# Swapping the two operands of a long convolution inside a gated attention and state-space kernel

## The chip, the core and the metric

The kernel runs on one core of a Trainium2 chip. The metric is the device time of one execution in microseconds. Three executions of the kernel before gave 949.06, 960.0 and 962.29 us, so their median is 960.0 us. The profiled execution is a fourth one and took 953.17 us.

## The reference, cut to what matters

```python
def reference(x, wqkv, wo, A, B, C, log_dt, Dskip, gate_w):      # x: 2048 x 512
    g = sigmoid((x * gate_w).sum(-1))
    a = attention(x, wqkv, 32 heads of 16) @ wo                   # softmax over all 2048 keys
    K[d, l] = Re sum_n C[d,n] * exp(dt[d]*A[d,n]*l) * dt[d]*B[d,n]   # 512 channels, 128 states
    y[l, d] = sum_{m<=l} K[d, m] * x[l-m, d]                      # causal, 2048 taps a channel
    return g * a + (1 - g) * (y + x * Dskip)
```

The reference does the convolution with Fourier transforms. The kernel does it directly, with matmuls.

## The kernel before, in words

Two problems share the core. **Attention** makes 2048 tiles of scores (4 heads side by side, 128 keys by 512 queries). A step, g, takes two or three of them: TensorE (PE) writes the scores into one of two PSUM tiles `SC0`, `SC1` (`qk`), ScalarE (ACT) takes their exponentials (`ex`, line 899, tile `ET`), and PE multiplies these by the values (`pv`, bank `OA`). There are 683 steps. From step 262 on VectorE (DVE) takes part of the exponentials with integer arithmetic (tiles `DZ`, `DU`), and a step then has two tiles on ACT and one on DVE. The queries for the next 16 steps come through `Qm` loads.

**The convolution** has two stages. The K stage (`table`, `kstage`) makes the 2048 taps of 32 channels, a block, 16 blocks in all: the tap at l = T*a + t is a product of a power for a and a power for t, summed over the states, so one matmul with 32 columns of `At` as weights and 64 or 48 columns of `PT` as moving operand makes them. T is 64: a runs over 32 partitions, t over 64 columns. `base_a`, `base_b`, `roots` and `factors` make the power tables on DVE (names beginning in L are small powers, in M large ones). The taps go out to DRAM (`kpd`) in rows of 2048 behind 32 zeros.

The Y stage (`ystage`) convolves. J = 32: output position l is cut into l = 32c + r, r on 32 partitions, c on 64 columns. For each channel 16 matmuls accumulate into bank `MB`: before, the weights are a 128 x 32 Toeplitz piece of the taps (`Kop`, loaded by `kloads` with overlapping rows, 8 channels to a load, three buffers) and the moving operand is the input `X` (32 channels a load, laid out with channels innermost, so that consecutive columns of one channel lie 32 elements apart). Four channels run side by side in the four column groups of the array: 512 matmuls a block, in groups of four. The bank `MB` is shared (a lock) by projections, K stage, Y stage and output projection.

**The order of the work** is written by a list scheduler in Python (`Sched`) while the program is recorded. It keeps a clock for each engine and adds a cost for each piece: `KMM` for a group of four K matmuls, `YMM` for a group of four Y matmuls, in us. After each step `fill` puts the waiting pieces of the other threads into the gaps that by these costs PE, DVE and the SP queue have; left-over gaps get matmuls on zeros (`wm`) that keep PE active. What is left when the steps have run out follows behind them. At run time each engine goes through its list strictly in order, so a matmul that waits holds up the scores behind it. All loads of both stages, and the `Qm` loads, go through the one SP queue in its order.

Of the kernel before, what the change touches and what calls it, by code (L numbers as in the profile page):

```python
# [13 lines left out]
P = 128  # L14
# [15 lines left out]
YAT = 140  # L30
XB = 32
XW = NC * XB
ZCOL = .216 / 512
# [24 lines left out]
VG = 4 * VW + 16  # L58
KMM = .055
YMM = .055  # L60
YSEG = 2
# [357 lines left out]
def declare(nc, es):  # L419
# [56 lines left out]
    for h in range(2):  # L476
        for n in ("L2", "L4", "L8", "L16", "L32", "L48", "M1", "M2", "M4", "M8", "M16", "M24", "W1"):
            sb(f"{n}.{h}", D, FP32)
        for n in (16, 32, 48):
            sb(f"DL{n}.{h}", 8 * D // 2)  # L480
        for n in (8, 16, 24):
            sb(f"DM{n}.{h}", 4 * D // 2)

# [10 lines left out]
    sb("sE", 16 * 32)  # L494
    sb("Kst", 2 * 512)
    for k in range(NK):
        sb(f"Kop{k}", KG * 512)
    for k in range(2):
        sb(f"X{k}", XW)
    sb("Yst", 2 * 512)  # L500
# [3 lines left out]
    B["MB"] = Buf("MB", "ps", 512, FP32)  # L504
    for n, free in (("kpd", D * KR), ("xrd", S * D), ("ytd", D * S), ("ybd", D * 512), ("qd", D * S), ("od", D * S)):
        B[n] = Buf(n, "dr", free, BF16)
        B[n].t = nc.dram_tensor("gm_" + n, [free // P, P], BF16)
# [95 lines left out]
def record(nc, p, B, ins):  # L603
# [51 lines left out]
    for n, s in (("BreT", "bre"), ("BimT", "bim"), ("CreT", "cre"), ("CimT", "cim")):  # L655
        load_par(n, ins[s])
    dma("SP", lambda e: e.dma_start(B["gwT"](0, [[1, 4]]), dap(ins["gw"], 0, [[1, P], [P, 4]]), allow_slow_non_contiguous=True),
        [], [(B["gwT"], 0)], lat=4)
    for k in range(D // XB):
        dma("SP", lambda e, k=k: e.dma_start(B["xrd"].dram(k * XW, [[XB, NC], [S * D // J, J], [1, XB]]),  # L660
                                             dap(x_t, (J - 1) * D + XB * k, [[J * D, NC], [-D, J], [1, XB]])), [], [(B["xrd"], k)], c=.6, lat=12)
    dma("SP", lambda e: e.dma_start(B["od"].dram(1536 * D, [[1, 512 * D]]), dap(x_t, 1536 * D, [[1, 512 * D]])), [], [(B["od"], 3)], c=.6, lat=6)
# [396 lines left out]
    def roots(h):  # L1059
        for o, x in (("L2", "L1"), ("L4", "L2"), ("L8", "L4")):  # L1060
            yield from cmul(o, x, x, h)
        for o, x, y in (("L16", "L8", "L8"), ("L32", "L16", "L16"), ("L48", "L16", "L32")):
# [4 lines left out]
        for o, x, y in (("M8", "M4", "M4"), ("M16", "M8", "M8"), ("M24", "M8", "M16")):  # L1067
            yield from cmul(o, x, y, h)
            yield from factors(o, h)

    def factors(n, h):
        l, d, z = B[f"{n}.{h}"], B[f"D{n}.{h}"], n[0] == "L"
# [53 lines left out]
    def base_a(pb):  # L1126
        At, h, d0 = B[f"At{pb}"], pb // 4, NP * (pb % 4)
        yield from powers(pb, FP, ((0, "W0"), (1, "W1")), ((2, "M2", None), (4, "M4", None)), True)
        yield ("DVE", .65)
        op("DVE", lambda v: v.tensor_copy(At(0, [[NA, 2], [2 * NA, NP], [1, 8]]), FP(0, [[e8, 2], [8, NP], [1, 8]])),  # L1130
           [(FP, 0)], [(At, 0)], c=.65)
        for m in range(1, 4):
            C = B[f"DM{8 * m}.{h}"]
            for ti, yr in ((v1, 0), (v2, 1)):
# [27 lines left out]
    def table(blk):  # L1162
# [8 lines left out]
        for m in range(1, 4):  # L1171
            Dm = B[f"DL{16 * m}.{h}"]
            for k in range(2):
# [10 lines left out]
    def skip():  # L1184
# [9 lines left out]
        yield ("SP", .6)  # L1194
        dma("SP", lambda e: e.dma_start(kpd.dram(0, [[4 * KR, P], [KR, 4], [1, J]]), wm(0, [[J, 4], [1, J]])), [(wm, 0)], [(kpd, "z")], c=.6, lat=4)

    def kstage(blk):
# [8 lines left out]
        for i in range(8):  # L1206
            yield ("PE", 4 * KMM)
            for x in range(2):
                for k in range(2):
                    n = T - 16 * k  # L1210
                    for j in range(4):
                        mm(lambda i=i, j=j, n=n: MB(64 * i + T - n, [[1, n]], 32 * j, 32),
                           lambda i=i, j=j, x=x: At(NA * (2 * (a0 + 4 * i + j) + x), [[1, NA]]),
                           lambda i=i, j=j, x=x, k=k, n=n: PT(k * PA + n * (2 * (4 * i + j) + x), [[1, n]]),
                           R, ky, False, x == k == 1, pos=(0, 32 * j), c=KMM if j == 0 else 0, a=n // 4, cfg="C")
        yield ("DVE", .7, -1)
        op("DVE", lambda v: v.tensor_copy(Kst(512 * (blk % 2), [[1, 512]]), MB(0, [[1, 512]])), ky, [(Kst, blk % 2, blk)], c=.66)  # L1217
# [9 lines left out]
    def kloads():  # L1227
        for v in range(D // KG):
            K, blk = B[f"Kop{v % NK}"], v * KG // CB
            yield ("AFTER", f"g{YAT}")  # L1230
            yield ("AFTER", f"kd{blk}")
            if v >= NK:
                yield ("AFTER", f"yv{v - NK}")
            for a in range(4):
                yield ("SP", .6)
                dma("SP", lambda e, a=a, v=v, K=K: e.dma_start(K(0, [[512, KG], [1, 512]], 32 * a, 32),  # L1236
                                                               kpd.dram(v * KG * KR + 1 + 512 * a, [[1, 32], [KR, KG], [1, 512]])),
                    [(kpd, (blk, j)) for j in range(4)] + [(kpd, "z")], [(K, a, v)], c=.62, lat=3.0)
            sch.mark(f"kl{v}")

    def xloads():
        yield ("AFTER", f"g{YAT}")
        for k in range(2):
            X = B[f"X{k}"]
            yield ("POOL", .3)
            op("POOL", lambda g, X=X: g.memset(X(0, [[1, XW]]), 0.0), [], [(X, a) for a in range(4)], c=4)
        for k in range(D // XB):
            X = B[f"X{k % 2}"]
            if k >= 2:
                yield ("AFTER", f"yu{XB * (k - 1) // CB - 1}")  # L1250
            for a in range(4):
                yield ("SP", .6)
                dma("SP", lambda e, a=a, k=k, X=X: e.dma_start(X(16 * a * XB, [[1, (NC - 16 * a) * XB]], 32 * a, 32),
                                                               B["xrd"].dram(k * XW, [[S * D // J, J], [1, (NC - 16 * a) * XB]])),
                    [(B["xrd"], k)], [(X, a, k)], c=.62, lat=3.0)
            sch.mark(f"xl{k}")

    Yst, ytd, ybd, Yl, Yb = B["Yst"], B["ytd"], B["ybd"], B["Yl"], B["Yb"]

    def ystage():  # L1260
        for u in range(NBLK):
            k, r2 = CB * u // XB, u % 2
            X = B[f"X{k % 2}"]
            yield ("AFTER", "gt")
            yield ("AFTER", f"xl{k}")
            yield ("AFTER", f"kl{CB * u // KG}")
            yield ("LOCK", "MB")
# [5 lines left out]
            for i in range(8):  # L1273
                v = (CB * u + 4 * i) // KG
                K = B[f"Kop{v % NK}"]
                R = [(K, a, v) for a in range(4)] + [(X, a, k) for a in range(4)]
                yield ("AFTER", f"kl{v}")
# [224 lines left out]

    for th, pr in ((norms(), 0), (qms(), 0), (projs(), 1), (gate(), .8), (ystage(), 2), (kloads(), 3), (space(), 2), (vscaled(0), 2.2), (vscaled(1), 2.2), (skip(), 1.9),
                   (xloads(), 4), (early(), 1.5), (reload(), 5), (outs(), 6)):
# [123 lines left out]
```

## Time and profile before

| | |
|---|---|
| profiled execution, device time | 953.17 us |
| its span, first to last instruction | 951.4 us |
| granted TensorE clock, mean | 0.937 |
| busy share: PE, DVE, ACT | 85%, 76%, 84% |
| exponential steps on ACT: first begins, last ends | 12.97 us, 866.8 us |

The span has three parts for this change. Up to step 140 (213.8 us) the convolution only makes tables. From step 140 its operands are loaded, and Y matmuls run among the steps. After the last step the rest of the convolution and the closing work run with ACT idle. Busy shares are means over all of these; what a stage costs has to be read in that stage.

### The profile page before, as it was taken

Reading aid. Unit: us, or ns where it says so; the run is one execution under the profiler, and the core shown is the slowest. Engines: PE = TensorE matmul, PEld = TensorE weight load, DVE = VectorE, ACT = ScalarE, POOL = GpSimd, SP = SyncE. Lnnn points to the kernel's source line nnn. Section 1 sums busy time; section 2 is a strip of 40 time slices with the busy share of each in tenths; the row PEclk is TensorE's granted clock in tenths of the full one; section 3 lists DMA queues with packets and bytes.
Section 4 is the critical chain, followed back from the end, with each engine's and each line's share of the span. In section 5 each row is a group of like instructions: output and inputs, shape, how many; then the busy total and the mean of one; then the engine's idle time right before and its main releaser. Section 6 shows DMA issues by size and latency. Waiting matters only on the chain.

```text
span 951.4 us, 35452 instructions
## 1 busy us (share of the span) xinstructions
PE 809.7 (85%) x16143; PEld 379.6 (40%) x16170; DVE 727.3 (76%) x1316; ACT 797.9 (84%) x694; POOL 13.4 (1%) x13
## 2 busy tenths in 40 slices
PE   7887777777888988998989989998999999999253
PEld 3222233322354555644544334343442444446150
DVE  5877999997969453786977989987899999983004
ACT  6996999999979886897979999997998999994000
POOL 5000000000000000000000000000000000000000
PEclk7877999999999998999989999999999999999676
DMA  8761000028175897776756414569553645456923
GB/s 188 73 52 8 16 11 13 16 56 185 38 164 117 173 189 147 165 143 132 159 120 132 81 33 94 112 110 170 113 116 75 143 99 114 97 116 138 172 59 112
DMA packets 202870, 101.10 MB, mean 106 GB/s; under 512 B 121424, under 2 KB 201168, under 8 KB 202704
## 3 DMA queue, kind: packets, MB, share of 16 engines
q1 hardware_dynamic: 200720, 97.65, 51.5%
q8 instruction: 127, 2.08, 1.0%
q10 hardware_dynamic: 2000, 1.18, 0.5%
q14 instruction: 23, 0.19, 0.1%
HBM read 83.40 MB, written 13.03 MB: 101 GB/s over the span
## 4 chain that ended last, share of the span: by engine, by line
PE 56%; ACT 28%; DMA 5%; DVE 4%; issue 4%; SPq 2%; ACTq 0%; DVEq 0%
ACT ET L899 28%; PE MB L619 25%; PE SC L619 16%; PE OA L619 15%; DMA gm_qd<-Qs 2%; DMA X<-gm_xrd 1%; SPq L1236 1%; DVE DZ L935 1%; DMA Wq<-in_A_wqkv_dram 1%; DVE OnT L989 1%; DMA Wo<-in_A_wo_dram 1%; DMA Kop<-gm_kpd 1%; DVE ON L982 0%; DMA Yl<-gm_ytd 0%; DVE DU L946 0%
## 5 line engine op out<-in xcount | busy, mean ns | idle before, releaser
L899 ACT ACTIVATE ET<-SC 128x1024 bf16<-128x1024 f32 (+1 forms) x683 | 789.9, 1337 | 65.2 <-PE SC L619 59.1
L619 PE MATMUL SC<-Qm,KT 32*128 32x512 bf16 x2048 | 281.4, 397 | 57.6 <-ACT ET L899 46.8
L619 PE MATMUL MB<-X,Kop 128*32 128x49 bf16 (+15 forms) x8192 | 269.7, 281 | 35.1 <-DMA X<-gm_xrd 17.3
L935 DVE TENSOR_SCALAR DZ<-SC 128x512 uint16<-128x512 f32 x340 | 227.2, 684 | 38.8 <-PE SC L619 35.3
L619 PEld LDWEIGHTS MB<-X,Kop 128*32 128x32 bf16 x8192 | 202.3, 111 | 91.2 <-issue 71.0
L619 PE MATMUL OA<-ET,VE 128*32 128x512 bf16 x1708 | 176.0, 405 | 2.8 <-issue 1.5
L619 PEld LDWEIGHTS SC<-Qm,KT 32*128 32x128 bf16 x2048 | 69.9, 91 | 256.9 <-ACT ET L899 166.8
L619 PE MATMUL OA<-wm 32*128 32x512 bf16 (+3 forms) x474 | 141.8, 410 | 2.3 <-DVE wm L671 1.2
L619 PEld LDWEIGHTS OA<-ET,VE 128*32 128x32 bf16 x1708 | 43.9, 94 | 101.3 <-issue 98.2
L1289 DVE TENSOR_TENSOR Yst<-MB,gt 128x512 bf16<-128x512 f32 x16 | 11.0, 687 | 89.9 <-PE MB L619 89.9
L1590 ACT CAST fo<-MB 128x512 bf16<-128x512 f32 x1 | 0.6, 585 | 77.8 <-PE MB L619 77.8
L946 DVE TENSOR_SCALAR DZ<-DZ 128x2048 uint16<-128x2048 uint16 x85 | 58.1, 684 | 7.3 <-PE OA L619 7.2
L946 DVE TENSOR_SCALAR DU<-DZ 128x2048 uint16<-128x2048 uint16 x85 | 58.0, 692 | 0.4
L970 DVE STREAM_TRANSPOSE OT<-OA 128x512 f32<-128x512 f32 x32 | 22.8, 711 | 19.5 <-PE OA L619 19.3
L619 PEld LDWEIGHTS OA<-wm 32*128 32x128 bf16 (+2 forms) x474 | 33.3, 94 | 9.2 <-issue 7.9
L619 PE MATMUL OA<-DZ,VS 128*32 128x512 bf16 x340 | 34.0, 389 | 0.9 <-DVE DZ L946 0.9
L619 PE MATMUL OA<-DU,VS 128*32 128x512 bf16 x340 | 33.7, 386 | 0.8 <-DVE DU L946 0.8
L619 PE MATMUL MB<-PT,At 128*32 128x64 bf16 (+1 forms) x2048 | 26.1, 192 | 9.0 <-issue 9.0
L619 PE MATMUL OA<-DZ,VE 128*32 128x512 bf16 x340 | 33.8, 388 | 0.0
L619 PEld LDWEIGHTS MB<-PT,At 128*32 128x32 bf16 x2048 | 23.6, 95 | 17.8 <-issue 13.6
L619 PE MATMUL MB<-Wo,OnT 128*128 128x512 bf16 x43 | 14.8, 413 | 16.7 <-DMA Wo<-in_A_wo_dram 14.7
L1217 DVE CAST Kst<-MB 128x512 bf16<-128x512 f32 x16 | 11.0, 686 | 22.9 <-PE MB L619 16.3
(220 smaller groups left out, 561.4 us busy)
## 6 DMA issues: line engine op xcount, KB each, us to landing
Kop<-gm_kpd SPq DMA_DIRECT2D x256, 256.0 KB, 5.4
gm_xrd<-in_A_x_dram SPq DMA_DIRECT2D x16, 128.0 KB, 5.5
gm_kpd<-Kst SPq DMA_DIRECT2D x64, 32.0 KB, 2.1
Wo<-in_A_wo_dram SPq DMA_DIRECT2D x4, 512.0 KB, 5.3
X<-gm_xrd SPq DMA_DIRECT2D x16, 128.0 KB, 4.9
gm_ytd<-Yst SPq DMA_DIRECT2D x16, 128.0 KB, 4.7
AR<-gm_od SPq DMA_DIRECT2D x8, 256.0 KB, 6.0
gm_qd<-Qs SPq DMA_DIRECT2D x15, 128.0 KB, 1.8
```

The costliest lines, as they stand in the source:

```text
L619: op("PE", lambda t: t.matmul(out(), lhsT(), rhs(), start=start, stop=stop, skip_group_check=True, **kw), R, W, c=c, lat=.15, a=a, cfg=cfg)
L899: op("ACT", lambda a: a.activation(ET(512 * e, [[1, 512 * n]]), sc(0, [[1, 512 * n]]), AF.Exp, scale=DH ** -0.5), [(sc, i, g) for i in ran ...
L935: op("DVE", lambda v: v.tensor_scalar(z.u16(512 * k, [[1, 512 * n]]), sc(512 * na, [[1, 512 * n]]), XS, XBI, ALU.mult, ALU.add), [(sc, na ...
L946: op("DVE", lambda v: v.tensor_scalar(t.u16(0, [[1, 2048]]), z.u16(0, [[1, 2048]]), float(STEP[k][0]), None, ALU.add), R, W, c=.07 + 2048 ...
L970: op("DVE", lambda v: v.transpose(OT(512 * w, [[1, 512]]), OA(0, [[1, 512]])), [(OA, 0, b)], [(OT, w, b)], c=.64)
L989: op("DVE", lambda v: v.transpose(OnT[qc](pi * 512, cols), ON(0, [[1, 512]])), [(ON, 0), (ON, 1)], [(OnT[qc], pi)], c=.64)
L1217: op("DVE", lambda v: v.tensor_copy(Kst(512 * (blk % 2), [[1, 512]]), MB(0, [[1, 512]])), ky, [(Kst, blk % 2, blk)], c=.66)
L1236: dma("SP", lambda e, a=a, v=v, K=K: e.dma_start(K(0, [[512, KG], [1, 512]], 32 * a, 32), kpd.dram(v * KG * KR + 1 + 512 * a, [[1, 32], [K ...
L1289: op("DVE", lambda v, r2=r2: v.tensor_tensor(Yst(r2 * 512, [[64, 8], [1, 64]]), MB(0, [[64, 8], [1, 64]]), B["gt"](0, [[0, 8], [1, 64]]), ...
L1590: op("ACT", lambda a, i=i, b=b, off=off: a.copy(fo(i * D, [[1, D]]), b(off, [[1, D]])), R, W, c=.5)
```

## The change

Input and taps change places in the Y stage. The input, now stored channel by channel with 32 zeros ahead (`xpd`), becomes the Toeplitz weights (`Xop`, the same load shape as `Kop` had). The taps become the moving operand (`Kf`, a whole block of 32 channels in one load, two buffers), with the 64 columns of a channel next to one another. For that the taps must come out of the K stage with r on the partitions and c on the columns, so the two tables change roles: powers 0 to 31 go to `At`, multiples of 32 to `PT`. `Kst` carries 48 zeros ahead of each channel's 64 taps, and its store (one instead of four) mirrors the 32 rows. The gather of x into `xrd` at the start falls away; four stores of the transposed input take its place. `KMM` goes from .055 to .03, `YMM` from .055 to .035, and the loading threads get other priorities.

```diff
-XB = 32
-XW = NC * XB
+KP = NC + 48
+KW = CB * KP
-KMM = .055
-YMM = .055
+KMM = .03
+YMM = .035
...
-    for k in range(D // XB):
-        dma("SP", lambda e, k=k: e.dma_start(B["xrd"].dram(k * XW, [[XB, NC], [S * D // J, J], [1, XB]]),
-                                             dap(x_t, (J - 1) * D + XB * k, [[J * D, NC], [-D, J], [1, XB]])), [], [(B["xrd"], k)], c=.6, lat=12)
...
-        for o, x, y, c in (("M1", "L32", "L32", 0), ("W1", "W0", "M1", 1), ("M2", "M1", "M1", 0), ("M4", "M2", "M2", 0)):
+        for o, x, y, c in (("M1", "L16", "L16", 0), ("W1", "W0", "L1", 1), ("M2", "M1", "M1", 0), ("M4", "M2", "M2", 0), ("M8", "M4", "M4", 0)):
...
-        yield from powers(pb, FP, ((1, "L1"),), ((2, "L2", None), (4, "L4", None), (8, "L8", B16)), False)
+        yield from powers(pb, FP, ((1, "M1"),), ((2, "M2", None), (4, "M4", None), (8, "M8", B16)), False)
...
-        for j in range(4):
-            yield ("SP", .6, 1)
-            dma("SP", lambda e, j=j: e.dma_start(kpd.dram((CB * blk + j) * KR + J, [[T, 32], [4 * KR, 8], [1, T]]),
-                                                 Kst(512 * (blk % 2), [[T, 8], [1, T]], 32 * j, 32)),
-                [(Kst, blk % 2, blk)], [(kpd, (blk, j))], c=.62, lat=3.0)
+        yield ("SP", .6, 1)
+        dma("SP", lambda e: e.dma_start(kpd.dram((J * blk + J - 1) * KW, [[8 * KP, 4], [-KW, J], [1, 8 * KP]]), Kst(r0, [[1, 8 * KP]])),
+            [(Kst, blk % 2, blk), (Kst, "z")], [(kpd, blk)], c=.62, lat=3.0)
...
+        yield ("AFTER", "K0.3")
+        for q4 in range(4):
+            yield ("SP", .6)
+            dma("SP", lambda e, q4=q4: e.dma_start(xpd.dram(P * q4 * KR + J, [[KR, P], [1, S]]), xT(q4 * S, [[1, S]])),
+                [xk(c, q4) for c in range(4)], [(xpd, q4)], c=.6, lat=6)
...
+                dma("SP", lambda e, a=a, v=v, X=X: e.dma_start(X(0, [[512, KG], [1, 512]], 32 * (3 - a), 32),
+                                                               xpd.dram(v * KG * KR + 1 + 512 * a, [[1, J], [KR, KG], [1, 512]])),
...
+            dma("SP", lambda e, k=k, K=K: e.dma_start(K(0, [[1, KW - 48]]), kpd.dram(J * k * KW, [[16, 4], [KW, J], [1, KW - 48]])),
+                [(kpd, k)], [(K, 0, k)], c=.62, lat=4.5)
...
-                               lambda i=i, j=j, A=A, K=K: K(((4 * i) % KG + j) * 512 + 32 * A, [[1, 32]]),
-                               lambda i=i, j=j, A=A, X=X, u=u: X((CB * u + 4 * i + j) % XB, [[XB, NC - A]]),
+                               lambda i=i, j=j, A=A, X=X: X(((4 * i) % KG + j) * 512 + J * A, [[1, J]]),
+                               lambda i=i, j=j, A=A, K=K: K((8 * j + i) * KP, [[1, NC - A]]),
```

The scheduler makes a new order from this. Three places of it follow. In the rows, `32x64 x4` is four matmuls with 64 moving columns, and the first name after the arrow is the moving operand.

PE before, around the scores of step 232, in the middle of the Y stage:

```order
L619 MATMUL MB<-X_193,Kop_189 32x62 x4
L619 MATMUL MB<-X_193,Kop_189 32x61 x4
L619 MATMUL SC<-Qm,KT 128x512
L619 MATMUL OA<-wm 128x512
L619 MATMUL SC<-Qm,KT 128x512 x2
L619 MATMUL OA<-ET,VE 32x512 x4
L619 MATMUL MB<-X_193,Kop_189 32x60 x4
```

PE after, around the scores of the same step:

```order
L619 MATMUL MB<-Kf_192,Xop_191 32x50 x4
L619 MATMUL MB<-Kf_192,Xop_191 32x49 x4
L619 MATMUL SC<-Qm,KT 128x512
L619 MATMUL OA<-wm 128x512
L619 MATMUL SC<-Qm,KT 128x512 x2
L619 MATMUL OA<-ET,VE 32x512 x4
L619 MATMUL MB<-Kf_192,Xop_191 32x64 x4
```

Between two scores there are 10 groups of Y matmuls before, and 16 after (a whole accumulation of four channels). Counted over the order, PE has 3056 Y matmuls between the scores of step 140 and those of step 290 before, 4096 after; 4048 behind step 290 among the steps before, 4096 after; and 1088 behind the last scores before, none after. After, Y matmuls begin at step 168 and end at step 575.

SP before, at the first reuse of the buffers (step 184 and on); `Kop0` to `Kop2` are the three buffers of the weights:

```order
L1236 DMA Kop2_191<-gm_kpd 32x8x512 x4
L1236 DMA Kop0_189<-gm_kpd 32x8x512 x2
L1294 DMA gm_ytd<-Yst_194 128x8x64
L1297 DMA gm_ybd<-Yst_194 128x8x16
L1236 DMA Kop0_189<-gm_kpd 32x8x512 x2
L1253 DMA X0_192<-gm_xrd 32x2048
L1253 DMA X0_192<-gm_xrd 32x1536
L1253 DMA X0_192<-gm_xrd 32x1024
L1253 DMA X0_192<-gm_xrd 32x512
```

SP after, at the first reuse of a tap buffer (step 177); `Kf0` is one of the two tap buffers, `Xop0` to `Xop2` the three weight buffers:

```order
L1241 DMA Xop2_191<-gm_xpd 32x8x512 x4
L1254 DMA Kf0_192<-gm_kpd 128x1x3536
L1293 DMA gm_ytd<-Yst_194 128x8x64
L1296 DMA gm_ybd<-Yst_194 128x8x16
L1241 DMA Xop0_189<-gm_xpd 32x8x512 x4
L1377 DMA gm_od<-AO0_75 128x4x512
L1241 DMA Xop1_190<-gm_xpd 32x8x512 x4
```

Four loads of the input on 32 partitions each become one load of taps on 128 partitions; the weight loads keep shape and number. A tap load stands behind the weight loads that were issued ahead of it, and is needed one block later.

PE before, behind the last scores:

```order
L619 MATMUL MB<-X_193,Kop_189 32x50 x4
L619 MATMUL MB<-X_193,Kop_189 32x49 x4
L619 MATMUL MB<-Yb,idb 128x512
L619 MATMUL MB<-Wo,OnT_73 128x512 x3
L619 MATMUL SC<-Yb,idb 128x512
```

PE after, behind the last scores:

```order
L619 MATMUL OA<-ET,VE 32x512 x4
L619 MATMUL OA<-wm 32x512 x4
L619 MATMUL MB<-Yb,idb 128x512
L619 MATMUL MB<-Wo,OnT_73 128x512 x3
L619 MATMUL SC<-Yb,idb 128x512
```

The closing output projection (`Yb`, `Wo`) stood behind the last Y matmuls and now stands behind the last value products. On ACT and DVE the order moves eight tiles of exponentials: DVE takes 87 sets of four tiles instead of 85.

More of the change, by code (lines that the diff above doesn't have):

```diff
@@ L494, in declare @@
     sb("sE", 16 * 32)
-    sb("Kst", 2 * 512)
+    sb("Kst", 2 * 8 * KP)
     for k in range(NK):
-        sb(f"Kop{k}", KG * 512)
+        sb(f"Xop{k}", KG * 512)
     for k in range(2):
-        sb(f"X{k}", XW)
+        sb(f"Kf{k}", KW)
     sb("Yst", 2 * 512)
@@ L504, in declare @@
     B["MB"] = Buf("MB", "ps", 512, FP32)
-    for n, free in (("kpd", D * KR), ("xrd", S * D), ("ytd", D * S), ("ybd", D * 512), ("qd", D * S), ("od", D * S)):
+    for n, free in (("kpd", J * D * KP), ("xpd", D * KR), ("ytd", D * S), ("ybd", D * 512), ("qd", D * S), ("od", D * S)):
         B[n] = Buf(n, "dr", free, BF16)
@@ L1127, in base_a @@
         At, h, d0 = B[f"At{pb}"], pb // 4, NP * (pb % 4)
[L1128 removed]
+        yield from powers(pb, FP, ((0, "W0"), (1, "W1")), ((2, "L2", None), (4, "L4", None)), True)
         yield ("DVE", .65)
@@ L1193, in skip @@
                                                  allow_slow_non_contiguous=True), [(sF, 0)], [(sF, 1 + k)], c=.6, lat=4)
-        yield ("SP", .6)
-        dma("SP", lambda e: e.dma_start(kpd.dram(0, [[4 * KR, P], [KR, 4], [1, J]]), wm(0, [[J, 4], [1, J]])), [(wm, 0)], [(kpd, "z")], c=.6, lat=4)
+        op("POOL", lambda g: g.memset(Kst(0, [[1, 16 * KP]]), 0.0), [], [(Kst, 0), (Kst, 1), (Kst, "z")], c=1.8)
     def kstage(blk):
@@ L1235, in kloads @@
                 yield ("SP", .6)
[L1236 to L1241, printed above, removed]
-        yield ("AFTER", f"g{YAT}")
[L1243 to L1248, printed above, removed]
-            if k >= 2:
[L1250 to L1256, printed above, removed]
+                dma("SP", lambda e, a=a, v=v, X=X: e.dma_start(X(0, [[512, KG], [1, 512]], 32 * (3 - a), 32),
+                                                               xpd.dram(v * KG * KR + 1 + 512 * a, [[1, J], [KR, KG], [1, 512]])),
+                    [(xpd, v * KG // P), (xpd, "z")], [(X, a, v)], c=.62, lat=3.0)
+            sch.mark(f"xl{v}")
+    def kloads():
+        yield ("AFTER", f"g{YAT}")
+        for k in range(NBLK):
+            K = B[f"Kf{k % 2}"]
+            yield ("AFTER", f"kd{k}")
+            if k >= 2:
+                yield ("AFTER", f"yu{k - 2}")
+            yield ("SP", .6)
+            dma("SP", lambda e, k=k, K=K: e.dma_start(K(0, [[1, KW - 48]]), kpd.dram(J * k * KW, [[16, 4], [KW, J], [1, KW - 48]])),
+                [(kpd, k)], [(K, 0, k)], c=.62, lat=4.5)
+            sch.mark(f"kl{k}")
     Yst, ytd, ybd, Yl, Yb = B["Yst"], B["ytd"], B["ybd"], B["Yl"], B["Yb"]
@@ L1274, in ystage @@
                 v = (CB * u + 4 * i) // KG
-                K = B[f"Kop{v % NK}"]
-                R = [(K, a, v) for a in range(4)] + [(X, a, k) for a in range(4)]
-                yield ("AFTER", f"kl{v}")
+                X = B[f"Xop{v % NK}"]
+                R = [(X, a, v) for a in range(4)] + [(K, 0, u)]
+                yield ("AFTER", f"xl{v}")
                 for A0 in range(0, 16, YSEG):
```

41 lines of the change are left out of this document (22 added, 19 removed).

## The prediction

> **What bounds the kernel now.** I read the page's busy shares and chain first, then ACT's idle time, and then cut the span into the stages before and after the last exponential.
>
> ```profile
> PE 809.7 (85%) x16143; PEld 379.6 (40%) x16170; DVE 727.3 (76%) x1316; ACT 797.9 (84%) x694; POOL 13.4 (1%) x13
> PE 56%; ACT 28%; DMA 5%; DVE 4%; issue 4%; SPq 2%; ACTq 0%; DVEq 0%
> L899 ACT ACTIVATE ET<-SC 128x1024 bf16<-128x1024 f32 (+1 forms) x683 | 789.9, 1337 | 65.2 <-PE SC L619 59.1
> 213.80:445.60 231.80, 203.18 (x4956) 113.70 (x4962) 161.34 (x323) 201.62 (x151) 0.00 (x0) 0.97 0.70 146
> 445.60:866.90 421.30, 401.43 (x7871) 174.14 (x7882) 372.58 (x607) 398.80 (x394) 0.00 (x0) 0.98 0.53 111
> 866.90:951.40 84.50, 36.96 (x1079) 29.33 (x1072) 11.89 (x14) 1.17 (x2) 0.00 (x0) 0.74 0.58 123
> ```
>
> The windows' columns are width, then busy time and instructions of PE, weight loads, DVE, ACT and POOL, the granted clock, DMA share and GB/s. Steps 140 to 290 are the first window (A), steps 290 to the end the second (B), the rest is the tail (C). ACT idles 30.2 us in A (231.8 - 201.6), 22.5 in B, and practically all of C's 84.5; what ends its idle time is the scores on PE. So ACT sets the least time of A and B, PE's excess stretches them, and C is what did not fit. C holds Y matmuls, waits for their loads, and the closing work:
>
> ```profile
> 905.22 9.04 PE L619 MATMUL MB<-X,Kop 128*32 128x64 bf16 x337 [13.15 <-DMA X<-gm_xrd]
> 880.05 5.86 issue
> 936.35 1.46 PE MB L619 x3
> 941.83 2.33 DVE OnT L989
> 945.25 1.21 ACTq L1356
> ```
>
> From 936.4 to 951.4 runs the closing chain (output projection, last normalisation, store): 15.0 us.
>
> **The Y matmuls.**
>
> ```profile
> L619 PE MATMUL MB<-X,Kop 128*32 128x64 bf16 x512 | 39.6, 289 | 19.8 <-DMA X<-gm_xrd 17.3 <-issue 1.3 <-DMA Kop<-gm_kpd 1.1
> L619 PE MATMUL MB<-PT,At 128*32 128x64 bf16 x1024 | 24.3, 194 | 6.7 <-issue 6.7
> 181.71 0.54 PE L619 MATMUL MB<-PT,At 128*32 128x64 bf16 x48
> ```
>
> A Y matmul lasts 289 ns but four run side by side and they are pipelined: 337 in 9.04 us, less one's 0.28, is 104 ns per group of four. The K matmul next to it has the same shape (128 rows, 32 weight columns, 64 or 48 moving columns) and differs in that its moving columns are adjacent: 48 in 0.54 us, less 0.19, is 29 ns per group. After the change Y has adjacent columns too, so I take 30 ns. That is 2048 x 74 ns = 152 us less PE time. The scheduler charged 55 ns for what took 104, which is where ACT's 52.7 us of idle time in A and B came from; with .035 it charges about what I expect, and puts all of Y among the steps.
>
> The Trainium skill speaks for and against. "SBUF — State Buffer", section Door 1, says that reads which go to a new 16-byte line each time pay a penalty; the 104 against 29 ns agree. "TensorE: Matmul & The Clock Gate", Part 1, gives a floor of about 25 ns between matmul starts however narrow they are; by that a group of four would stay at 100 ns and nothing would be won. The 48 matmuls in 0.54 us contradict it here for matmuls that lie side by side in the array.
>
> **Tail: -69.5.** After, Y ends at step 575 and its stores and the final adds lie among the last hundred steps. C keeps the closing 15.0 us: -69.5. Should some of the output adds run late, a few us come back; one store's landing bounds that.
>
> **Stage A: the loads.** Here the cover goes. The plan takes 8 blocks of Y between steps 168 and 290, the inner ones 13 to 15 steps each, some 18 us. What can be loaded?
>
> ```profile
> 875.00:880.00 5.00, 3.77 (x127) 3.35 (x127) 0.00 (x0) 0.00 (x0) 0.00 (x0) 1.00 1.09 225
> Kop<-gm_kpd SPq DMA_DIRECT2D x256, 256.0 KB, 5.4
> X<-gm_xrd SPq DMA_DIRECT2D x16, 128.0 KB, 4.9
> 948.40:949.20 0.80, 0.00 (x0) 0.00 (x0) 0.00 (x0) 0.00 (x0) 0.00 (x0) 0.50 0.53 184
> out_dram<-fo SPq DMA_DIRECT2D x2, 128.0 KB
> Qm<-gm_qd SPq DMA_DIRECT2D x120, 16.0 KB, 2.1
> 119.20 137.13 ACT ET L899 x102
> ```
>
> With only `Kop` loads in flight the core moves 225 GB/s. A block's 16 weight loads are 4.19 MB, 19 us: already more than the plan gives. Before, PE was too slow to notice (1.1 us of waits on `Kop`). The tap load adds to it, and its shape matters. The final stores `out<-fo` have an outermost dimension of 8 in DRAM, and while they alone run the DMA share is 0.53, eight of 16 engines, at 184/8.5 = 21.7 GB/s each. `Kf` and the store of `Kst` have an outermost 4 on the DRAM side, so I estimate 4 engines: 226 KB of taps on each of the four. At 21.7 GB/s that is 10.4 us, at 225/16 = 14.1 GB/s it is 16.1; I take 13.2. The same four carry their share of the weights (262 KB: 12.1 to 18.6, taken 15.5), of `Kst` (0.75 stores a block in A, 43 KB: 2.0 to 3.1, taken 2.5) and of the small Y transfers (1.5). So a block costs F = 13.2 for the taps and O = 19.5 for the rest.
>
> The Trainium skill, "DMA: Bandwidth & Descriptors", section on why a DMA increments its semaphore by 16, gives the rule behind the 0.53: a copy is spread over the largest number up to 16 that divides both outermost dimensions, 4 here. By it F would be 10 to 16; without it 905 KB at 225 GB/s is 4.0.
>
> Loads start at step 140; three weight loads and two tap loads fit the buffers, and then nothing moves until step 168, 28 steps of 137.13/102 = 1.34 us (the chain's longest stretch on ACT), 38 us, later. After that 7.25 blocks of O and 6 of F are to be loaded while PE works: 38 + 7.25 x 19.5 + 6 x 13.2 = 258 us, against 231.8 now: **+26**. A Y matmul that waits for `Xop` or `Kf` holds up the scores behind it in PE's list, and ACT runs dry once the two score tiles are used; now ACT waits there for slow Y matmuls instead. With the low ends (O 15.6, F 10.4) it is 213, -19; with the high ends (O 23.2, F 16.1) 303, +71. ACT's 201.6 lies below all. The first block's own wait is covered by the 38 us.
>
> **Stage B: -11.** Eight blocks need 8 x 32.7 = 262 us of loading; steps 290 to 575, which hold them, lie at 447 to 757 us now, so loading is covered on average. Waits where Y is dense, and fetches of instructions on PE, keep half of the 22.5 us: -11. Bounds: -22.5; and +12 if a block needs 40 us (8 x 40 = 322 against 310).
>
> ```profile
> 319.07 1.87 issue
> L899 ACT ACTIVATE ET<-SC 128x1536 bf16<-128x1536 f32 x342 | 472.8, 1619 | 46.0 <-PE SC L619 43.6 <-PE OA L619 1.6
> L899 ACT ACTIVATE ET<-SC 128x1024 bf16<-128x1024 f32 x341 | 324.6, 1054 | 19.2 <-PE SC L619 15.5 <-PE OA L619 2.8
> L946 DVE TENSOR_SCALAR DU<-DZ 128x2048 uint16<-128x2048 uint16 x85 | 58.0, 692 | 0.4
> L935 DVE TENSOR_SCALAR DZ<-SC 128x512 uint16<-128x512 f32 x340 | 227.2, 684 | 38.8 <-PE SC L619 35.3
> 24.50 27.46 SPq L660 DMA_DIRECT2D gm_xrd<-in_A_x_dram  x16
> 61.93 14.30 DMA gm_qd<-Qs
> ```
>
> **Small edits.** Eight tiles leave ACT for DVE: an exponential of three tiles keeps ACT busy 472.8/342 = 1.38 us and one of two 324.6/341 = 0.95, so 8 x 0.43 = **-3.4**. DVE gains 8 x 0.68 plus four wide ones of 0.69, 8 us on 372.6 in B, and stays below ACT's 398.8. The power tables have the same number of multiplications: 0; two blocks of them move into A, where DVE has 70 us free. The sixteen gathers of x leave SP and its 27 us; four 512 KB stores come before the gate's small stores. The first `Qs` store waits 14.3 us to land, and I cannot say whether it waits for the gather or for the small stores behind it: 0, between -12 and +12. The `Kst` copy now writes steps of 64 columns: 0, 16 instructions of 0.69 us off the path. Zeroing `Kst` on POOL is early: 0.
>
> **Sum**, against the profiled execution's 951.4 + 1.8 outside the span: 951.4 - 69.5 + 26 - 11 - 3.4 + 1.8 = 895 us. The low ends give 951.4 - 69.5 - 19 - 22.5 - 3.4 + 1.8 = 839, the high ends 951.4 - 69.5 + 71 + 12 - 3.4 + 1.8 = 963. The profiled 953.2 is 0.7% under the median of 960.0; a measurement of this kernel tells about 2% from no change, so the limits are 941 and 979.
>
> **Rivals.** *Forecast: the loads pace stage A* (870 to 945, predicted 895), 0.54. For it: 4.19 MB per 18 us is more than any row with `Kop` shows. I put 0.06 of this above 941.
>
> *The loads keep up* (0.22): the taps run on 16 engines (F 4.0, O 22.5: 38 + 163 + 24 = 225, so -7), or four engines hold 21.7 GB/s (-19), and B loses its idle time: 839 to 851. For it: low ends are seen in this trace. Against: `Kop` streams stay near 225.
>
> *The queue serialises* (0.18): `Qm` loads, four every 16 steps, stand on SP behind three weight loads and a tap load, and land through the same four engines. If PE waits for each tap load with its buffers drained, a block costs 19 + 16 + 5 = 40 us with nothing overlapped, and with the buffers idle while `Qm` is awaited some 42: A 38 + 7.25 x 26 + 6 x 16 = 322 (+90), B 8 x 42 - 310 = +26: 951.4 - 69.5 + 90 + 26 - 3.4 + 1.8 = 996, slower. It decides from about 40 us a block, where the sum passes the old time. Against: now `Qm` lands in some 2 us. Of the 0.18, 0.03 stay within 2%.
>
> *The swap does not speed the matmul* (0.06): weights, not columns, hold a group at 104 ns. Then 2048 x (104 - 35) ns = 141 us overrun the plan; before 1776 groups x 49 = 87 us cost 52.7 us of ACT, 0.6 of it, so 85 now: 951.4 - 69.5 + 85 - 52.7 - 3.4 + 1.8 = 913. The `PT` rows speak against it. The floor that the Trainium skill states in "TensorE: Matmul & The Clock Gate", Part 1, would lead to this case.
>
> Faster: 0.48 + 0.22 + 0.06 = 0.76; same 0.06 + 0.03 = 0.09; slower 0.15. The range 830 to 970 leaves out the serialised queue's slow end, 0.15, and little below the low ends.
>
> **What would show it.** Right: groups of four Y matmuls some 30 ns apart; nothing but the closing 15 us behind the last exponential; in stage A idle time of PE ended by loads of `Xop` and `Kf`, and DMA at its limit; landing of `Kf` far above its planned 4.5 us, 13 or more. Wrong: `Kf` landing in 5 us and A at ACT's pace (then 840); PE waiting for `Qm` at block starts (then slower); the granted clock falling in A because PE pauses there, which I priced at nothing.

## The result and the profile after

The change made the kernel slower: 1043.5 us (median of four) against 956.8 for the kernel before on the same chip, ratio 1.091 (95% interval 1.081 to 1.101). The forecast was 895 with a range of 830 to 970, so it was wrong in its sign. The profiled execution took 1040.1 us, span 1038.3.

The page of the kernel after, busy shares, the chain by engine and by line, and the costliest groups:

```profile
PE 735.9 (71%) x16255; PEld 287.0 (28%) x16285; DVE 732.4 (71%) x1328; ACT 792.2 (76%) x694; POOL 11.5 (1%) x12
...
ACT 31%; PE 23%; SPq 17%; DMA 12%; issue 9%; DVE 7%; ACTq 0%; DVEq 0%
...
L896 ACT ACTIVATE ET<-SC 128x1024 bf16<-128x1024 f32 (+1 forms) x683 | 784.3, 1376 | 228.1 <-PE SC L619 222.9
...
L619 PE MATMUL MB<-Kf,Xop 128*32 128x55 bf16 (+15 forms) x8192 | 121.4, 204 | 160.5 <-issue 82.2
```

PE had 56% of the chain before and has 23% now; the SP queue went from 2% to 17%, DMA from 5 to 12, "issue" from 4 to 9. ACT does the same work (792 us) and waits 223 us for scores instead of 59. The stages, cut at the same steps as before (columns as there):

```profile
212.70:534.30 321.60, 194.81 (x6299) 92.77 (x6301) 181.71 (x363) 200.52 (x151) 0.00 (x0) 0.75 0.70 155
534.30:1024.50 490.20, 378.22 (x7693) 131.32 (x7684) 364.95 (x587) 395.47 (x394) 0.00 (x0) 0.87 0.52 103
1024.50:1038.30 13.80, 5.39 (x27) 1.94 (x24) 5.17 (x7) 1.17 (x2) 0.00 (x0) 0.75 0.12 39
```

The tail is gone, 84.5 to 13.8 us. Stage A grew from 231.8 to 321.6 and B from 421.3 to 490.2, with ACT idle for 121 and 95 us; the granted clock fell from 0.97 to 0.75 in A.

One block of the Y stage on the SP queue (start, duration, line, transfer):

```profile
350.14 0.53 SPq L1254 DMA_DIRECT2D Kf<-gm_kpd  x1
350.71 0.52 SPq L1293 DMA_DIRECT2D gm_ytd<-Yst  x1
351.28 10.37 SPq L1296 DMA_DIRECT2D gm_ybd<-Yst  x1
361.69 4.46 SPq L1241 DMA_DIRECT2D Xop<-gm_xpd  x3
...
383.54 0.53 SPq L1254 DMA_DIRECT2D Kf<-gm_kpd  x1
384.11 0.49 SPq L1293 DMA_DIRECT2D gm_ytd<-Yst  x1
384.64 9.43 SPq L1296 DMA_DIRECT2D gm_ybd<-Yst  x1
394.11 5.49 SPq L1241 DMA_DIRECT2D Xop<-gm_xpd  x3
```

Behind these tap loads SP stands some 10 us in one issue, that of a 32 KB store which took 0.71 us in the kernel before. Nothing behind it starts. Two stretches ahead of this standing and in it show the DMA (last two columns):

```profile
345.00:351.00 6.00, 3.67 (x143) 1.95 (x143) 1.15 (x2) 2.44 (x3) 0.00 (x0) 0.62 1.13 223
355.00:362.00 7.00, 7.00 (x257) 3.59 (x248) 3.94 (x8) 5.65 (x5) 0.00 (x0) 0.64 0.28 104
```

With weight loads in flight all 16 engines work at 223 GB/s. With the tap load alone the share is 0.28, a little over four engines, at 104 GB/s. PE and ACT are busy then, with scores, K matmuls and Y matmuls whose weights are still in the buffers; afterwards PE has drained them. (In the rows, x64 is the number of matmuls, and the brackets hold the wait ahead of them.)

```profile
262.24 0.68 PE L619 MATMUL MB<-Kf,Xop 128*32 128x54 bf16 x64
...
366.25 0.40 PE L619 MATMUL OA<-ET,VE 128*32 128x512 bf16 x4
371.08 0.95 PE L619 MATMUL MB<-Kf,Xop 128*32 128x64 bf16 x64 [4.43 <-DMA Xop<-gm_xpd]
...
372.91 0.67 PE L619 MATMUL MB<-Kf,Xop 128*32 128x64 bf16 x36
376.90 0.50 PE L619 MATMUL MB<-Kf,Xop 128*32 128x55 bf16 x28 [3.32 <-issue]
```

Two sorts of wait stand here: for weights, and "issue", in which PE waits for nothing that the profile names. The waits of the whole execution (total, times, longest):

```profile
PEld MB L619 <- issue: 234.3, 311, 16.6
ACT ET L896 <- PE SC L619: 222.9, 115, 16.9
...
PE MB L619 <- DMA Xop<-gm_xpd: 78.1, 16, 10.3
```

### The profile page after: what moved, and what is told of

Same layout as the page of the kernel before. It is cut to its first block, busy times and chain, and to the rows that moved or that the text cites. A ratio compares the mean times of both kernels' runs of the same rounds, so it can differ in the third digit from the quotient of the medians.

```text
span 1038.3 us, 35559 instructions
## 1 busy us (share of the span) xinstructions
PE 735.9 (71%) x16255; PEld 287.0 (28%) x16285; DVE 732.4 (71%) x1328; ACT 792.2 (76%) x694; POOL 11.5 (1%) x12
## 4 chain that ended last, share of the span: by engine, by line
ACT 31%; PE 23%; SPq 17%; DMA 12%; issue 9%; DVE 7%; ACTq 0%; DVEq 0%
ACT ET L896 31%; SPq L1296 9%; PE SC L619 8%; PE OA L619 8%; DMA Xop<-gm_xpd 8%; PE MB L619 7%; SPq L1241 6%; DMA gm_qd<-Qs 2%; DMA Qm<-gm_qd 2%; DVE DZ L932 2%; SPq L1306 1%; SPq L1303 1%; DMA Wq<-in_A_wqkv_dram 1%; DVE ft L989 1%; DVE DU L943 1%
## 5 line engine op out<-in xcount | busy, mean ns | idle before, releaser
L619 PE MATMUL SC<-Qm,KT 32*128 32x512 bf16 x2048 | 306.6, 428 | 96.9 <-ACT ET L896 68.5
L619 PE MATMUL MB<-Kf,Xop 128*32 128x55 bf16 (+15 forms) x8192 | 121.4, 204 | 160.5 <-issue 82.2
L619 PE MATMUL OA<-ET,VE 128*32 128x512 bf16 x1700 | 187.5, 433 | 6.4 <-issue 4.9
L619 PEld LDWEIGHTS MB<-Kf,Xop 128*32 128x32 bf16 x8192 | 102.9, 105 | 212.9 <-issue 192.2
L619 PE MATMUL OA<-wm 32*128 32x512 bf16 (+3 forms) x565 | 159.5, 420 | 1.2 <-DVE wm L668 1.2
L619 PE MATMUL OA<-DZ,VE 128*32 128x512 bf16 x348 | 38.4, 431 | 0.0
L619 PE MATMUL OA<-DU,VS 128*32 128x512 bf16 x348 | 37.5, 421 | 1.0 <-DVE DU L943 1.0
L619 PE MATMUL MB<-xT,Wq 128*128 128x512 bf16 x50 | 16.9, 417 | 11.4 <-DVE Qs L705 10.0
L989 DVE TENSOR_TENSOR FP<-ft,ft 128x128 f32<-128x128 f32 (+1 forms) x64 | 22.8, 356 | 1.8
```

The lines of the kernel that those rows point to most:

```text
L619: op("PE", lambda t: t.matmul(out(), lhsT(), rhs(), start=start, stop=stop, skip_group_check=True, **kw), R, W, c=c, lat=.15, a=a, cfg=cfg)
L989: op(eng, lambda v: v.tensor_tensor(o(), a(), b_(), f), R, W, c=c)
```

## The experiments

Theory N: the tap load, on four engines, is what makes a block some 36 us long. Its rivals were V, the volume of the loads however they are spread, and P, PE's own list of instructions and the clock. Every ratio below is against the kernel before on the same chip.

### Taps on 16 engines

```diff
-            dma("SP", lambda e, k=k, K=K: e.dma_start(K(0, [[1, KW - 48]]), kpd.dram(J * k * KW, [[16, 4], [KW, J], [1, KW - 48]])),
+            for a in range(4):
+                dma("SP", lambda e, k=k, K=K, a=a: e.dma_start(K(0, [[1, KW - 48]], 32 * a, 32), kpd.dram(J * k * KW + 16 * a, [[KW, J], [1, KW - 48]])),
...
```

> The changed kernel, with each tap load cut into four loads of 32 partitions each, whose outermost dimension in DRAM is 32 instead of 4; bytes, place in the order and everything else as they were. Theory N (the narrow load): the tap load runs on four engines, SP stands some 10 us behind it in each block (10.2, 9.4, 10.4, 9.4 us in the blocks of stage A), and the weight loads behind it start late. Then the long standing goes, a tap load lands in 4 to 6 us, a block of stage A takes 25 to 29 us instead of 36, and the time falls by 8 blocks x 8 us in A and 30 to 60 us in B, to 900 to 950 us. Theory V (the volume: 5.3 MB a block in 18 planned us, however spread): blocks get shorter by 3 us at most, 1000 to 1040 us. Theory P (PE's own list: fetches of instructions and the lower granted clock): within 20 us of 1043.

Measured: 973.0 us, ratio 1.024 (1.017 to 1.031): 70 us less than the kernel after. SP at the same place:

```profile
338.26 3.07 SPq L1255 DMA_DIRECT2D Kf<-gm_kpd  x4
341.38 0.42 SPq L1294 DMA_DIRECT2D gm_ytd<-Yst  x1
341.85 0.57 SPq L1297 DMA_DIRECT2D gm_ybd<-Yst  x1
342.47 4.64 SPq L1241 DMA_DIRECT2D Xop<-gm_xpd  x3
```

and from the page of this kernel ACT's waits and the landing of the four parts:

```profile
L896 ACT ACTIVATE ET<-SC 128x1024 bf16<-128x1024 f32 (+1 forms) x683 | 786.2, 1348 | 159.6 <-PE SC L619 153.9
...
Kf<-gm_kpd SPq DMA_DIRECT2D x64, 221.0 KB, 5.5
```

The standing is gone, taps land in 5.5 us, and the dense blocks take 29 to 34 us (from one multiplication by the gate, `Yst`, to the next: 273.0, 306.7, 338.0, 367.3, 396.7 us). So N is shown for 70 us, though the gain is smaller than expected; V and P alone would have left the time above 1000 us. PE's waits for weights, 78.1 us in the kernel after, are gone:

```profile
PE MB L619 <- DMA Xop<-gm_xpd: 2.7, 1, 2.7
```

Yet ACT still waits 154 us. In stage A these waits now have nearly one cause. PE stands without a named reason, for example here (timeline of PE):

```profile
293.17 0.40 PE L619 MATMUL OA<-ET,VE 128*32 128x512 bf16 x4
293.40 0.64 PE L619 MATMUL MB<-Kf,Xop 128*32 128x64 bf16 x59
299.33 0.27 PE L619 MATMUL MB<-Kf,Xop 128*32 128x50 bf16 x5 [5.29 <-issue]
```

PE's instructions in the trace (matmuls, weight loads and the few that only handle semaphores) can be numbered in their order. The instructions behind gaps over 1 us between 293 and 369 us, with gap, number, and remainder by 256:

```
5.29 us  7616  192      2.44 us  9152  192      2.01 us 10432  192
1.57 us  8128  192      1.50 us  9664  192      1.87 us 10688  192
4.14 us  8384  192      1.79 us  9920  192      1.68 us 11200  192
                        2.76 us 10176  192
```

All stand at the same place of a piece of 256. In the DMA records PE's queue of instructions has packets of 16 KB, 1.3 us each here, and PE goes on a median of 1.45 us after one has landed. Between 290 and 535 us there are 36 such stands of over 0.3 us, 79.2 us together, and 3 gaps elsewhere, 1.1 us. PE waits for its own program. (Records missing from a trace shift the numbers, so such sums are lower bounds.)

### No tap loads, and hardly any loads

Two kernels leave loads out, so their outputs are not the convolution; only their times matter here. The first takes the taps of later blocks from the first two:

```diff
+            if k < 2:
                 dma("SP", lambda e, k=k, K=K: e.dma_start(K(0, [[1, KW - 48]]), kpd.dram(J * k * KW, [[16, 4], [KW, J], [1, KW - 48]])),
...
-                R = [(X, a, v) for a in range(4)] + [(K, 0, u)]
+                R = [(X, a, v) for a in range(4)] + [(K, 0, u % 2)]
```

> The changed kernel without the tap loads after the first two: later blocks multiply by the taps of the first two (14 of 16 tap loads, 12.7 MB, are left out, and the result is wrong by that). All else stays, the weight loads too. Theory N: as with a tap load on 16 engines and 4 us better a block: blocks of 21 to 25 us, 870 to 920 us. Theory V: 4.4 MB a block remain of 5.3, so blocks shrink by a sixth, 36 to 30 us: 960 to 990 us. Theory P: 1000 us or more.

Measured: 941.4 us, ratio 0.991 (0.987 to 0.996). Between N's and V's numbers: without 12.7 MB of taps the time is 32 us below that of taps on 16 engines, so volume counts too. The second also leaves out the weight loads after the first twelve, beside the tap loads:

```diff
+                if v < NK:
                     dma("SP", lambda e, a=a, v=v, X=X: e.dma_start(X(0, [[512, KG], [1, 512]], 32 * (3 - a), 32),
```

> The changed kernel without the tap loads after the first two and without the weight loads after the first twelve (three buffers): later blocks multiply by what the buffers hold (14 of 16 tap loads and 244 of 256 weight loads, 77 MB, are left out; the result is wrong by that). Question: in the kernel with tap loads on 16 engines PE stands, between steps 192 and 330, almost only at every 256th instruction of its list (36 stands, 79 us), which then goes on 1.45 us after a fetch of 16 KB of instructions. Theory I-fixed (the fetch has its own turn-around, some 4 us, and PE goes through 256 instructions faster than that wherever Y matmuls are dense): the stands remain though hardly any data moves, 60 us or more in all, 900 to 940 us. Theory I-queue (the fetch waits behind data): the stands shrink below 20 us, 835 to 870 us. Theory V (waits for the loads themselves): as I-queue, 835 to 870 us, but then stands at other positions vanish, which tap16 hardly has.

Measured: 872.8 us (two executions, 868.5 and 877.2), ratio 0.914 (0.907 to 0.922). Its stages and page:

```profile
210.20:456.80 246.60, 178.29 (x6906) 91.06 (x6909) 182.58 (x364) 199.61 (x151) 0.00 (x0) 0.91 0.20 46
456.80:852.60 395.80, 344.17 (x7102) 122.18 (x7102) 358.46 (x579) 389.81 (x394) 0.00 (x0) 0.99 0.14 31
```

```profile
L896 ACT ACTIVATE ET<-SC 128x1024 bf16<-128x1024 f32 (+1 forms) x683 | 777.5, 1418 | 63.5 <-PE SC L619 61.5
...
L619 PE MATMUL MB<-Kf,Xop 128*32 128x58 bf16 (+15 forms) x8192 | 105.8, 193 | 42.9 <-issue 42.8
```

Neither half of theory I (the fetch of instructions, by its own time or by waiting behind data) had it alone. At a DMA share of 0.20, 31 stands at the fetch position remain in A, 41.6 us, where ACT idles 47 us. But each is shorter: the median over the execution is 1.36 us, against 1.85 with taps on 16 engines. The longest "issue" wait of a weight load goes the same way. With almost no loads:

```profile
PEld MB L619 <- issue: 106.0, 267, 2.3
```

with taps on 16 engines:

```profile
PEld MB L619 <- issue: 193.0, 324, 5.4
```

and 16.6 in the kernel after, in whose records one fetch of 16 KB takes 13.8 us. So the fetch has a turn-around of its own that dense Y matmuls outrun, and it is longer where more data is in flight. The volume costs time mainly in this way: PE waits for weights 2.7 us with taps on 16 engines and 1.7 us without the tap loads, while the stands at fetches add up to at least 123 and 97 us, and to some 47 us with almost no loads. The Trainium skill, "DMA: Bandwidth & Descriptors", section "Queues, rings and completion order", says that an engine serves its queues in turn, a whole packet from each; that would let data delay a fetch, but no record here shows the turns themselves.

In steps: 1043 with everything, 973 without the narrowness, 941 without the taps, 873 without the weights. The last two kernels also have a somewhat different order, since loads that aren't there take no time in the scheduler's plan: Y matmuls end at step 569 and 493 instead of 575, so they are denser, not thinner.

### The narrow load from another queue

```diff
-            yield ("SP", .6)
-            dma("SP", lambda e, k=k, K=K: e.dma_start(K(0, [[1, KW - 48]]), kpd.dram(J * k * KW, [[16, 4], [KW, J], [1, KW - 48]])),
+            yield ("POOL", .6)
+            dma("POOL", lambda e, k=k, K=K: e.dma_start(K(0, [[1, KW - 48]]), kpd.dram(J * k * KW, [[16, 4], [KW, J], [1, KW - 48]])),
```

> The changed kernel with the tap load, narrow as it is, issued by POOL instead of SP; all else as it was. It takes apart the two halves of the narrow load: that four engines carry the taps (my forecast's O + F on the same four engines, 32.7 us a block), and that SP stands behind it some 10 us a block and issues nothing for the other twelve. Theory N1 (the four engines' own time): weight loads still need their share on the same four engines, a block stays 31 to 36 us, 1010 to 1045 us. Theory N2 (SP standing): SP goes on issuing, the other twelve engines work beside the taps, a block takes 27 to 30 us and the time comes near that of the taps on 16 engines (973): 965 to 1000 us.

Measured: 1034.0 us, ratio 1.083 (1.078 to 1.089), in N1's range. The tap load lands in 18.9 us, and SP stands all the same, here at the next weight loads:

```profile
352.57 1.59 SPq L1296 DMA_DIRECT2D gm_ybd<-Yst  x1
354.20 13.41 SPq L1241 DMA_DIRECT2D Xop<-gm_xpd  x2
367.66 2.31 SPq L724 DMA_DIRECT2D Qm<-gm_qd  x4
```

```profile
Kf<-gm_kpd POOLq DMA_DIRECT2D x16, 884.0 KB, 18.9
```

So the queue that issues the narrow load hardly matters: SP stands behind it from another queue too. For the same reason the run can't tell N1 from N2, because SP never went on issuing as N2 supposed. What the standing costs beside the four engines' own time stays open.

### Spreading the blocks

If loads and fetches only need time, the Y stage can be given more steps. One line lets block u begin no earlier than step 168 + 27u:

```diff
             yield ("AFTER", "gt")
+            yield ("AFTER", f"g{168 + 27 * u}")
```

> The changed kernel with one line more: block u of the Y stage may not begin before step 168 + 27u, so that the 16 blocks spread over steps 168 to 675 instead of 168 to 575; loads keep their shapes. Theory N and theory V both: with 27 steps (36 us in A, 26 us in B) a block's 36 us of loading lie behind exponentials in A; ACT's idle time in A falls from 121 to below 50 us, B gains less because 27 steps there are 26 us: 900 to 980 us. Theory P: the stalls come with the matmuls wherever they stand: 1020 us or more.

Measured: 989.3 us, ratio 1.045 (1.036 to 1.055), a little above the expected range, below P's. ACT's idle time is 48 us in A, as expected, and 109 in B, more than the 95 of the kernel after.

Both together, taps on 16 engines and this line:

> Both: tap loads cut in four, and blocks begun no earlier than step 168 + 27u. Theory N: loading takes 25 to 28 us a block, the plan gives 36 in A and 26 in B, so ACT idles 10 to 40 us over A and B: 850 to 890 us, below the kernel before. Theory V: the blocks keep some 33 us: 890 to 940 us. Theory P: above 1000 us.

Measured: 950.3 us, ratio 0.999 (0.996 to 1.003). N's and V's ranges both missed it: idle 45 us in A and 76 in B. A block is still dense inside, 16 groups to a step, so the stands at fetches stay (49 of them, 102 us). Next, every piece of two groups has its own earliest step, with the taps on 16 engines and two weight buffers (`NK = 2`) instead of three:

```diff
+                    yield ("AFTER", f"g{150 + int(0.35 * (64 * u + 8 * i + A0 // YSEG))}")
                     yield ("PE", YSEG * YMM)
```

> Tap loads cut in four, and the Y matmuls spread: each piece of two groups (eight matmuls) may not begin before step 150 + 0.35 x its number, so that some six groups stand between two scores instead of 16; two weight buffers instead of three, since tables live longer and the room is gone. Data and matmuls as before. Theory I-fixed and I-queue: 256 instructions take 3.5 to 4 us instead of 2.3, stands at fetches fall from 123 us to 30 to 60: 870 to 920 us. Theory V: the loading thread is spread too, so the same gain, but then waits for Xop go and not stands at fetches; with two buffers they may even grow: 930 to 980 us.

Measured: 941.1 us, ratio 0.985 (0.978 to 0.991), some 1.5% less than the kernel before, which is within the 2% that the prediction takes for no change. Its waits:

```profile
ACT ET L896 <- PE SC L619: 109.4, 84, 8.0
...
PE MB L619 <- DMA Xop<-gm_xpd: 33.1, 17, 6.5
```

Stands at fetches fell to 67 us, near theory I, and waits for weights rose to 33. The time is 20 us above I's range and within V's, which had named these waits for two buffers. The edit does less than expected: in the trace the first three blocks still have 10 to 22 groups of Y matmuls in a step, and behind them the mean over the steps that hold any is 7, against 9 with taps on 16 engines alone.

```diff
-                    yield ("AFTER", f"g{150 + int(0.35 * (64 * u + 8 * i + A0 // YSEG))}")
+                    yield ("AFTER", f"g{160 + int(0.4 * (64 * u + 8 * i + A0 // YSEG))}")
```

> The same with 160 + 0.40 x number: five groups between two scores until step 352, some of the last block left behind the last step. Theory I: stands at fetches below those of 150 + 0.35, 20 to 50 us, and 5 to 10 us of tail: 870 to 920 us. Theory V: 930 to 980 us.

Measured: 942.8 us, ratio 0.988 (0.984 to 0.992). The time is again in V's range. Stands are 55 us and waits for weights 40; in A ACT idles 25 us only, but 49 us pass behind the last exponential, more than expected.

The control for both has the taps on 16 engines, two buffers and no spreading:

```diff
-NK = 3
+NK = 2
```

> Control for the two: tap loads cut in four and two weight buffers, Y matmuls as dense as the scheduler puts them. If two buffers cost nothing: within 20 us of the 973 us of three buffers, with as many stands at fetches (100 us or more). If two buffers are what loads cannot bear: 1000 us or more, with waits for Xop.

Measured once: 965.7 us, so the time is no longer with two buffers in the dense order. But PE's waits for `Xop` are 35.4 us here, against 2.7 with three buffers (and 4.1 in the paced kernel with taps on 16 engines, which has three too). As far as these runs show, the waits for weights in the spread kernels go with the two buffers and not with the spreading. No run spread the pieces with three buffers.

Then the spread of 160 + 0.40 with a lower charge:

```diff
-YMM = .035
+YMM = .025
```

> As the spread of 160 + 0.40 x number (tap loads cut in four, two weight buffers), with a charge of .025 us for a group of four Y matmuls instead of .035, so that no Y matmul is left behind the last step (the order has 512 there without it): Y matmuls between the scores of 32 steps are 728 at most, 16 in a step nowhere. Theory I: stands at fetches as there (some 55 us), its tail of 49 us falls to 15 to 25 us, some of it comes back among the steps because the charge is below what a group takes: 905 to 935 us. Theory V: waits for Xop grow by what the tail loses: 940 us or more.

Measured: 956.9 us, ratio 1.005 (1.001 to 1.008). Wrong for theory I: the tail shrank by 29 us to 20, but B's idle time rose from 59 to 98. The time is in V's range, yet waits for `Xop` grew by 10 us only (40 to 50), where V expected what the tail lost. So they are a part of it, and the rest isn't explained. The order wasn't as thin as expected either: between steps 203 and 211 six steps have 10 to 26 groups.

```diff
-YAT = 140
+YAT = 110
...
+                    yield ("AFTER", f"g{130 + int(0.4 * (64 * u + 8 * i + A0 // YSEG))}")
```

> As the spread of 150 + 0.35 x number (tap loads cut in four, two weight buffers), but loads may begin at step 110 instead of 140 and piece number n not before step 130 + 0.40 n: Y has 20 steps more, and the last block ends near step 620 with nothing behind the last step. What the earlier spreads cost: 941 us, with ACT idle for 38 us in A, 67 us in B and 25 us behind the last step. If the loads and the fetches of instructions want time and not another order, 27 us more of it take 10 to 30 us off: 905 to 935 us. If the waits come wherever Y matmuls stand: 935 to 945 us.

Measured: 952.6 us, ratio 0.997 (0.994 to 1.001), outside what either answer expected; idle 45 us in A and 76 in B. More room alone doesn't help. The scheduler put 1088 Y matmuls into the 32 steps from step 192 on, but it did so with 150 + 0.35 too, so this does not explain the 11 us between the two.

```diff
-YAT = 140
+YAT = 125
...
+                    yield ("AFTER", f"g{140 + int(0.38 * (64 * u + 8 * i + A0 // YSEG))}")
```

> The same with loads from step 125 and 140 + 0.38 n: later and, until step 330, somewhat thinner (800 Y matmuls in the scores of steps 224 to 255 instead of 880), with the last block close to the end (136 in the last eleven steps). Between the spread of 150 + 0.35 n and the one from step 110: 915 to 940 us.

Measured: 939.4 us, ratio 0.985 (0.978 to 0.992), at the upper end of what was expected, and the best found together with that of 150 + 0.35. What would bring these orders near the 873 of the kernel without loads stays open.

## Why the prediction was wrong, step by step

**The matmul: right.** 64 Y matmuls in 0.68 us, less 0.19, are 31 ns a group, as forecast. At 371 us the same takes 0.95 us, 48 ns, where the granted clock is 0.50 instead of 1.00. The floor of about 25 ns between matmul starts, which the Trainium skill states in "TensorE: Matmul & The Clock Gate", Part 1, does not hold for these matmuls side by side: 64 of them take 0.68 us.

**The tail: right.** -70.7 us against -69.5.

**Stage A: the step that failed first**, +26 forecast, +90 measured. Two of its parts were right. Four engines carry the taps (share 0.28). This agrees with the rule cited from the Trainium skill, "DMA: Bandwidth & Descriptors", section on why a DMA increments its semaphore by 16. And F was not too small: with nothing else in flight a 7072-byte row takes 272 ns, so four engines move 104 GB/s and 905 KB takes 8.7 us, less than the low end of 10.4. (Beside other rows a whole tap load took 10.2 to 16.8 us from its first row to its last.) What failed is the covering and the overlap around these costs, and a term that the sum lacks. The stage's 321.6 us are 49.6 to step 168, 16.4 to the first `Yst`, 254.2 for seven blocks and 1.4 behind them. The forecast had 38 for the first, nothing for the second, and 220 for the rest:

- The 38 us from step 140 to step 168 took 50. The first two tap loads, 26 us on their four engines, stood in SP's order ahead of a store of queries, for which the chain of the kernel after then waits; with taps on 16 engines these steps take 42 us. The chain at that place:

```profile
245.67 1.67 SPq L1241
247.44 7.78 DMA gm_qd<-Qs
```

- The first block's own wait was called covered. It took 16 us (step 168 at 262.3, its `Yst` at 278.7) that the sum doesn't have.
- Then "7.25 x 19.5 + 6 x 13.2" assumes that loading never pauses. The blocks took 36.3 us on average (`Yst` at 278.7 and, seven blocks on, at 532.9; 254 us) where the sum's terms give 32.7 and, with two tap loads ahead, 30.4. DMA's share in A is 0.70: while the taps run, the other twelve engines mostly idle (share 0.28 above). That loading also pauses while PE stands for instructions and frees no buffer is my reading; no run separates it.
- The sum has no term for the fetch of instructions. Without loads stage A still takes 246.6 us where the low end of the sum had 213, and 42 us of that are stands at fetches. Before, 32 groups of Y matmuls, which are 256 instructions, took 3.3 us, and such stands came to 16 us in all; at 30 ns a group they take 1.0 us, less than the fetch of a piece.

**Stage B: wrong**, -11 forecast, +69 measured. The step that failed is "loading is covered on average". Without loads B takes 395.8 us, even less than the low end's 398.8, so all that is above it came with the loads: 38 us with the weights (433.6), 27 with the taps on 16 engines (460.5), 30 with the narrow taps (490.2). An average over 310 us hides nothing here, because the scheduler puts the Y matmuls of each block into 14 to 21 steps, and a matmul that waits inside them holds up the scores at once. Behind each of the seven tap loads of B SP stands 9 to 13 us: in the 32 KB store five times, once in the queries' load and once in a load of Y results.

**Small edits: right.** ACT's busy time in A and B fell by 4.4 us (forecast 3.4), step 140 comes 1.1 us earlier (forecast 0, within 12), DVE bounds nothing.

**The granted clock, priced at nothing**, fell to 0.75 in A. It is 0.78 with taps on 16 engines, 0.81 without the tap loads and 0.91 without loads, with the same matmuls, so it goes with the time that PE stands. The prediction had named this as a sign of being wrong. How much of the 90 us it costs by itself wasn't separated.

**The rivals.** "The queue serialises" was nearest: slower, 996 us, with blocks of 40 us. But queries awaited at each block start were not the mechanism: such a wait is large once in the chain (17.3 us at 642.9). The four engines and the instruction fetch were. "The loads keep up" got its 839 to 851 not even with the loads left out (873). The chance of 0.15 for slower was too small, since the forecast and the rivals that counted had the loads as the one new bound; the fetch of instructions was named only as half of B's idle time.

## What to carry to other kernels

Work that becomes three times as fast takes its data and its instructions three times as fast: look at what is fed to it in the densest stretch, not on average, and include the engine's own program. For each new transfer look first at how many engines carry it (the outermost dimension on both sides); here a load on four of 16 held up SP's transfers behind it, whether SP's queue or POOL's had issued it. When work becomes cheap, a scheduler that fills gaps packs it more densely, and what feeds it has less time: here spreading it again, with two weight buffers, took the ratio from 1.024 to 0.985, but not to the forecast.

## What the runs showed of the hardware that was not expected

- PE's list arrives in pieces of 256 instructions (16 KB, 0.9 to 1.3 us each). Where Y matmuls were dense PE stood at the border of pieces, 1.36 us in the median with hardly any loads and 1.85 with loads, up to 5.3 us, and went on some 1.45 us after the piece had landed.
- A load on four engines with nothing beside it moved 104 GB/s, 26 GB/s an engine (7072 bytes in 272 ns; 321 ns in the median of all such rows), more than the 21.7 and 14.1 that the kernel before showed for other shapes.
- An issue of a 32 KB store stood 8.6 to 11.6 us behind a narrow 905 KB load, against 0.6 to 0.7 us, once 2.1, in the kernel before; with the load on POOL's queue SP stood as well (13.4 us for two weight loads).
